# Local attention in groups of 128 queries instead of 96: small TensorE tiles per chunk, sums taken after the values, one turn at the end

## The chip, the cores and the metric

The kernel runs on one core of a Trainium2 chip. The metric is device microseconds of one execution, from three runs of the kernel before. One further execution was profiled; all rows below come from it.

## What is computed

Three stages follow one another: chunked local attention, a two-matrix MLP, and a gated MLP. Cut to what matters:

```python
B, H, S, D = 4, 8, 768, 64;  chunk, left, right, n_mem = 32, 16, 8, 8
for c in range(S // chunk):                     # 24 chunks of 32 queries per batch and head
    k_full = concat(mem_k, k[c*32-16 : c*32+40])        # 8 + at most 56 keys = 64
    v_full = concat(mem_v, v[c*32-16 : c*32+40])
    s = q[chunk] @ k_full.T / sqrt(D);  a = exp(s - max(s))
    out[chunk] = (a / (sum(a) + 1e-9)) @ v_full
x = out as [3072 tokens, 512]
g = s * relu(x @ w_in)**2 + b;  y = g @ w_out           # d_ff 2048
out = (silu(y @ w_gate) * (y @ w_val)) @ w_out2         # d_ff 1536
```

All inputs and the output are float32.

## The kernel before

**Tiling.** The 3072 tokens are cut into 8 blocks of T = 384 for the first MLP. A block takes 4 attention groups of GQ = 96 queries, so there are 32 groups. A group covers 3 chunks; it loads 96 query rows and GK = 128 key and value rows (8 memory rows and 120 of the sequence), all 8 heads side by side, from DRAM in pieces of 64 floats (256 bytes).

**One group.** `stage_transposes` turns keys (4 transposes, two heads each, 128 columns) and queries (4 transposes, 96 columns) into PSUM. `stage_keys` copies both to SBUF. `stage_scores` makes 8 products, one per head, 64 rows deep, 96 queries against all 128 keys; a head of even number sits in TensorE's rows 0 to 63, one of odd number in rows 64 to 127. `stage_max` adds a mask that leaves each query its own 64 keys and takes the maximum, head by head. `stage_exp` takes the exponential head by head on ScalarE, with the sum. `stage_normalise` divides on VectorE. `stage_probs` turns the probabilities (8 transposes of 96 columns), `stage_probs_copy` copies them, `stage_values` multiplies by the values (8 products, 128 rows deep, 64 output rows each, two heads one above the other in PSUM). `stage_x` writes the result as two float32r halves, high and low.

**Passes.** A float32 product goes to TensorE as two passes, each with its own weight load; so 8 products are 16 records in a profile. A float32 transpose is one. The MLPs use float32r, three products for one (L422 to L424).

**The first MLP.** For each block and each of 16 slices m of d_ff: an up step (12 matmuls of 384 columns into `hp`), then relu, square, scale and rounding on ScalarE and VectorE, and a down step (12 matmuls into four banks `acc`). Block 0 is cut: m 0 to 5 of block 0, then all of block 1, then the rest of block 0, then blocks 2 to 7. Each slice's weights (1 MB) are loaded once and split into two float32r parts, mainly on VectorE (`split`); all 16 stay in SBUF.

**The order** is made when the program is built. `START` is the order of TensorE's first steps, written out by hand (T transposes, S scores, A probabilities, V values, U up, D down). Later groups are put between up and down steps by `tick`. `LOADS` is the order of the first transfers on the one DMA queue (SP). `MOVED` names the steps that may run on either of ScalarE and VectorE and are put on the second choice. `Plan.run` orders every engine's instructions from given lengths; TensorE keeps the order of the calls. On the chip each engine runs its list in order and waits for semaphores. The first nine groups are in `START`; the probabilities of the first 8 groups lie in three buffers lent from the weights. In PSUM attention has two banks `a`, and at the start also the `acc` banks.

The lines the steps below touch: L283 to L298 loads, L313 and L315 transposes, L333 scores, L354 maximum, L366 exponential, L376 division, L385 and L402 probabilities and values, L415 the low half, L222 and L224 copies, L233 and L238 weight loads, L482 and L484 rounding in the first MLP.

## Time and profile before

| what | value |
|---|---|
| median of 3 runs | 1258.27 us (1257.05 to 1258.80) |
| the profiled execution | 1259.23 us, its span 1257.5 us |
| TensorE busy | 1225.2 us, 97% of the span |
| VectorE, ScalarE busy | 761.3 us (61%), 625.9 us (50%) |
| granted TensorE clock, mean | 0.995 |
| moved by DMA | 171.84 MB in 157138 packets, 97512 of them under 512 bytes |

A busy share is taken over the whole span, though the stages have different limits. The time of a TensorE step is read here from start to start, since each matmul's record is longer than the distance to the next (they are pipelined). "PEld" is the weight load that belongs to a matmul.

### The profile page before, as it was taken

What the parts mean: (1) busy time and instruction counts of PE and PEld (TensorE: products, weight loads), DVE (VectorE), ACT (ScalarE), POOL (GpSimd) and SP (SyncE); (2) the same over time, 40 slices, a digit from 0 to 9 for tenths busy, and PEclk for the clock granted to TensorE, in tenths of its full rate; (3) what the DMA queues carried; (4) which work ended last, traced back from release to release, by engine and by line L of the source; (5) the groups of instructions that cost most, each with busy time, mean ns of one, the idle gap of its engine ahead of it and who ended that gap; (6) DMA issues with size and microseconds to landing.
All of it is one profiled execution on the core that took longest, in us unless ns stands there. A gap on an engine that the chain in (4) does not pass through costs nothing.

```text
span 1257.5 us, 22202 instructions
## 1 busy us (share of the span) xinstructions
PE 1225.2 (97%) x8496; PEld 1162.8 (92%) x8496; DVE 761.3 (61%) x1846; ACT 625.9 (50%) x1596; POOL 0.7 (0%) x6
## 2 busy tenths in 40 slices
PE   5899999999999999999999999999999999999998
PEld 4788999999999999999999999999999999999997
DVE  6989865444444444454569886667964447744444
ACT  6967455454454545453348554455543335433332
POOL 0000000000000000000000000000000000000000
PEclk9889999999999999999999999999999999999999
DMA  9973232222112122120263455567665558545532
GB/s 192 270 207 114 72 75 55 61 43 57 39 32 64 32 64 44 36 68 1 87 233 109 141 186 187 188 229 283 244 219 190 185 185 297 206 184 187 188 120 93
DMA packets 157138, 171.84 MB, mean 137 GB/s; under 512 B 97512, under 2 KB 128744, under 8 KB 155496
## 3 DMA queue, kind: packets, MB, share of 16 engines
q1 hardware_dynamic: 157032, 170.42, 42.7%
q8 instruction: 67, 1.10, 0.4%
q14 instruction: 39, 0.32, 0.1%
HBM read 122.42 MB, written 47.97 MB: 136 GB/s over the span
## 4 chain that ended last, share of the span: by engine, by line
PE 89%; DVE 6%; ACT 2%; DMA 1%; issue 1%; SPq 0%; DVEq 0%; ACTq 0%
PE hp L422 7%; PE acc L423 6%; PE acc L422 6%; PE acc L424 6%; PE hp L423 6%; PE hp L424 6%; PE chain_a L422 5%; PE chain_a L423 5%; PE chain_a L424 5%; PE oacc L423 5%; PE oacc L422 5%; PE oacc L424 5%; PE chain_b L423 4%; PE chain_b L422 4%; PE chain_b L424 4%; PE psS L333 3%
## 5 line engine op out<-in xcount | busy, mean ns | idle before, releaser
L422 PE MATMUL hp<-xhi,w_first 128*128 128x384 f32 x512 | 177.9, 347 | 0.0
L423 PE MATMUL acc<-glo,w_first 128*128 128x384 f32 x512 | 172.3, 337 | 4.7 <-DVE glo L482 4.5
L422 PE MATMUL acc<-ghi,w_first 128*128 128x384 f32 x512 | 173.0, 338 | 2.1 <-ACT kq L222 1.3
L424 PE MATMUL acc<-ghi,w_first 128*128 128x384 f32 x512 | 172.1, 336 | 0.0
L423 PE MATMUL hp<-xlo,w_first 128*128 128x384 f32 x512 | 171.5, 335 | 0.1
L424 PE MATMUL hp<-xhi,w_first 128*128 128x384 f32 x512 | 171.3, 335 | 0.0
L610 ACT ACTIVATE kept<-chain_a 128x256 f32<-128x256 f32 x216 | 83.0, 385 | 159.5 <-PE chain_a L424 132.2
L462 DVE SCALAR_TENSOR_TENSOR r<-r,s_sb 128x384 f32<-128x384 f32 x99 | 61.0, 616 | 143.2 <-ACT r L451 143.0
L451 ACT ACTIVATE r<-hp 128x384 f32<-128x384 f32 x116 | 56.7, 488 | 126.2 <-PE hp L424 125.2
L422 PE MATMUL oacc<-w_down,ghi 128*128 128x512 f32 x288 | 114.1, 396 | 0.1
L423 PE MATMUL oacc<-w_down,ghi 128*128 128x512 f32 x288 | 114.1, 396 | 0.0
L424 PE MATMUL oacc<-w_down,glo 128*128 128x512 f32 x288 | 112.0, 389 | 0.0
L366 ACT ACTIVATE sc<-sc,mx 96x128 f32<-96x128 f32 x256 | 99.3, 392 | 22.6 <-DVE mx L361 22.5
L484 DVE SCALAR_TENSOR_TENSOR glo<-r,b_sb,ghi 128x384 fp32r<-128x384 f32 x99 | 61.1, 617 | 68.5 <-ACT ghi L473 68.3
L423 PEld LDWEIGHTS acc<-glo,w_first 128*128 128x128 f32 x512 | 96.7, 189 | 6.1 <-DVE glo L482 5.5
L422 PEld LDWEIGHTS acc<-ghi,w_first 128*128 128x128 f32 x512 | 96.6, 189 | 3.4 <-ACT kq L222 1.5
L422 PEld LDWEIGHTS hp<-xhi,w_first 128*128 128x128 f32 x512 | 96.4, 188 | 3.0
L423 PEld LDWEIGHTS hp<-xlo,w_first 128*128 128x128 f32 x512 | 96.5, 188 | 0.3 <-DVE xlo L415 0.3
L424 PEld LDWEIGHTS acc<-ghi,w_first 128*128 128x128 f32 x512 | 96.7, 189 | 0.0
L424 PEld LDWEIGHTS hp<-xhi,w_first 128*128 128x128 f32 x512 | 96.2, 188 | 0.0
L627 DVE TENSOR_TENSOR v<-v,g 128x256 f32<-128x256 f32 x144 | 60.9, 423 | 56.5 <-ACT g L623 54.6
L473 ACT ACTIVATE ghi<-r,b_sb 128x384 fp32r<-128x384 f32 x95 | 58.3, 614 | 52.6 <-DVE r L462 51.5
(135 smaller groups left out, 2891.1 us busy)
## 6 DMA issues: line engine op xcount, KB each, us to landing
y<-ops_dram SPq DMA_DIRECT2D x48, 512.0 KB
ops_dram<-y SPq DMA_DIRECT2D x24, 512.0 KB
sum_dram<-o SPq DMA_DIRECT2D x48, 256.0 KB
o<-sum_dram SPq DMA_DIRECT2D x12, 1024.0 KB
yhi<-ops_dram_hi SPq DMA_DIRECT2D x12, 768.0 KB
ylo<-ops_dram_lo SPq DMA_DIRECT2D x12, 768.0 KB
raw_first<-in_moe_w_in_dram SPq DMA_DIRECT2D x16, 512.0 KB
raw_first<-in_moe_w_out_dram SPq DMA_DIRECT2D x16, 512.0 KB
```

Source lines behind the costliest of these rows:

```text
L333: nc.tensor.matmul(banks[e][:GQ, j * GK:(j + 1) * GK], qt[r, j, :], kt[r, j, :], start=True, stop=True)
L366: nc.scalar.activation(out=sc[:, h, :], in_=sc[:, h, :], func=AF.Exp, bias=mx[:, h:h + 1], scale=SCALE, accum_out=sm[:, h:h + 1],)
L422: nc.tensor.matmul(o, whi, xhi, start=first, stop=False, skip_group_check=onto)
L423: nc.tensor.matmul(o, whi, xlo, start=False, stop=False, skip_group_check=onto)
L424: nc.tensor.matmul(o, wlo, xhi, start=False, stop=last, skip_group_check=onto)
L451: nc.scalar.activation(out=r, in_=hp, func=AF.Relu)
L462: nc.vector.scalar_tensor_tensor(out=r, in0=r, scalar=s_sb[:, 0:1], in1=r, op0=ALU.mult, op1=ALU.mult)
L473: nc.scalar.activation(out=hi, in_=r, func=AF.Identity, bias=bias)
L484: nc.vector.scalar_tensor_tensor(out=lo, in0=r, scalar=bias, in1=hi.bitcast(F32), op0=ALU.add, op1=ALU.subtract)
L610: nc.scalar.activation(out=t, in_=st2[n]["A"], func=AF.Copy)
L627: nc.vector.tensor_tensor(out=v, in0=v, in1=g, op=ALU.mult)
```

## The change

A group now has 128 queries (4 chunks), so a block of 384 tokens takes 3 groups and there are 24. Keys come as 128 rows `ka` and 24 + 8 rows `kb`, and are transposed in pairs `ka`, `kb`; the copy to SBUF lays out, for each chunk, its own 64 keys (`stage_keys_copy`, twice for the sequence and twice for the memory rows). Scores: for each pair of heads, chunk and head a product of 64 rows by 32 queries by 64 keys, so 32 of them, in eight places of TensorE (2 by rows, 4 by columns). No mask is needed; the maximum is taken over four heads at once, then subtracted, and one exponential covers the group (two groups, g3 and g7, keep the old form with bias). Probabilities are turned 4 times 128 columns. Values: each chunk's 64 value rows are loaded to their own place (8 transfers of 56 rows by 4 heads, a column of ones beside each head), and 32 products give output and sum together, queries on partitions. The output is divided by the sum (`stage_sums`, `stage_normalise`), and a last step turns it (`stage_turn`, 4 transposes of 128 columns). `START`, `LOADS`, `MOVED` are new, and `VISITS` names the half steps at which a group's six TensorE steps come.

```diff
-GQ = 96
-GK = 128
+GQ = 128
 START = (
-    "T0 S0 T1 S1 T2 S2 A0 V0 A1 T3 S3 V1 T4 A2 V2 S4 T5 A3 V3 S5 U T6 A4 S6 V4 T7 U S7 A5 V5 T8 "
-    "D U D A6 U V6 D U D U A7 V7 D U D S8 U"
+    "Q0 T0 S0 Q1 T1 A0 V0 X0 S1 Q2 T2 A1 S2 V1 A2 X1 V2 X2 Q3 T3 U S3 U Q4 A3 D T4 U S4 D V3 "
+    "U Q5 A4 D X3 V4 U T5 D S5 U D A5 X4 V5 D X5 U "
 )
+VISITS = {
+    (True, 0): (-3, 3, 5, 7, 8, 15),
...
+    (False, 0): (-4, -2, 0, 2, 3, 10),
...
 LOADS = (
-    "K0 K1 W0 V0 K2 K3 W2 V2 K4 V1 K5 W1 V4 V3 W3 K6 K7 V5 W9 W4 K8 W5 V8 V6 W6 V7 W8 W10 W7 W11"
+    "W0 K0 W2 K1 V0 W1 K2 V1 W4 V2 K3 W3 K4 W5 W8 W6 V3 K5 V4 W7 W9 V5 W10 "
 )
...
-    T = 4 * GQ
+    T = 3 * GQ
...
+            for c in range(NC):
+                a = s0 + c * CHUNK - LEFT
...
+                        nc.sync.dma_start(
+                            out=tv[r0:r0 + n, c, :, 0:D],
+                            in_=v[b, e:H:2, first:first + n, :].rearrange("h s d -> s h d"),
+                        )
...
+    def stage_keys(g, early):
+        ka, kb = loaded[g]["ka"], loaded[g]["kb"]
+        n = REST + NMEM
+        for i in range(2):
...
+            for jj in range(2):
+                c = slice((2 * i + jj) * P, (2 * i + jj + 1) * P)
+                nc.tensor.transpose(kps[:, jj, 0:P], ka[:, c], ident)
+                nc.tensor.transpose(kps[:, jj, P:], kb[:n, c], ident[:n, :n])
...
         for j in range(NP):
-            for e in range(2):
-                r = slice(e * D, (e + 1) * D)
-                nc.tensor.matmul(
-                    banks[e][:GQ, j * GK:(j + 1) * GK], qt[r, j, :], kt[r, j, :], start=True, stop=True
-                )
+            for c in range(NC):
+                cs = slice(c * CHUNK, (c + 1) * CHUNK)
+                for e in range(2):
+                    r = slice(e * D, (e + 1) * D)
+                    nc.tensor.matmul(banks[e][cs, j], qt[r, j, cs], kt[r, j, c], start=True, stop=True)
...
-            nc.vector.tensor_tensor_reduce(
-                out=sc[:, h, :], in0=banks[e][:GQ, j * GK:(j + 1) * GK], in1=mask, scale=1.0,
-                scalar=BIG, op0=ALU.add, op1=ALU.max, accum_out=mx[:, h:h + 1],
-            )
+        nc.vector.tensor_reduce(
+            out=staged[g]["mx"][:, e].rearrange("p j o -> p (j o)"), in_=ps, op=ALU.max, axis=AX.X
+        )
...
+        nc.scalar.activation(out=sc, in_=sc, func=AF.Exp, scale=SCALE)
...
-        for h in range(H):
-            j, e = divmod(h, 2)
-            nc.tensor.matmul(vps[e * D:(e + 1) * D, j, :], tv[:, h, :], at[:, h, :], start=True, stop=True)
+        for j in range(NP):
+            for c in range(NC):
+                cs = slice(c * CHUNK, (c + 1) * CHUNK)
+                for e in range(2):
+                    r = slice(e * KC, (e + 1) * KC)
+                    nc.tensor.matmul(banks[e][cs, j], at[r, j, cs], tv[r, c, j], start=True, stop=True)
...
+    def stage_turn(g):
+        on = staged.pop(g)["on"]
+        vps = bank(ps_h, "h", f"psO{g}").rearrange("p (j s) -> p j s", j=NP)
+        for j in range(NP):
+            nc.tensor.transpose(vps[:, j, :], on[:, j].rearrange("p e d -> p (e d)"), ident)
```

On TensorE in the first MLP, a later group's key step stood between a down and an up step like this before (`ident` is the identity, `x4` four in a row; sizes are output rows by columns):

```order
L424 MATMUL acc_1258<-ghi,w_first_1625 128x384
L313 MATMUL psT_0_1864<-ident,k_920 128x128 x4
L315 MATMUL psT_1_1865<-ident,q_923 128x96 x4
L422 MATMUL hp<-xhi_402,w_first_1148 128x384
```

and like this now:

```order
L500 MATMUL hp<-xhi_411,w_first_1502 128x384
L361 MATMUL psK_0_2370<-ident,ka_2065 128x128
L362 MATMUL psK_0_2370<-ident,kb_2066 128x32
L361 MATMUL psK_0_2370<-ident,ka_2065 128x128
L362 MATMUL psK_0_2370<-ident,kb_2066 128x32
L361 MATMUL psK_1_2375<-ident,ka_2065 128x128
L362 MATMUL psK_1_2375<-ident,kb_2066 128x32
L361 MATMUL psK_1_2375<-ident,ka_2065 128x128
L362 MATMUL psK_1_2375<-ident,kb_2066 128x32
L498 MATMUL acc_2203<-ghi,w_first_1463 128x384
```

The queries have moved to a step of their own, and transposes from all 128 rows alternate with transposes from 32 rows (`kb`).

On TensorE in a scores step, one product per head stood in a row before, even heads to bank 0 and odd heads to bank 1:

```order
L333 MATMUL psS_0_209<-kq_0_205,kq_0_207 96x128
L333 MATMUL psS_1_210<-kq_0_205,kq_0_207 96x128
L333 MATMUL psS_0_209<-kq_0_205,kq_0_207 96x128
L333 MATMUL psS_1_210<-kq_0_205,kq_0_207 96x128
```

and now, of 32 rows the first eight (four chunks, even and odd head of one pair):

```order
L390 MATMUL psS_0_1148<-kt_1110,qt_986 32x64
L390 MATMUL psS_1_1149<-kt_1110,qt_986 32x64
L390 MATMUL psS_0_1148<-kt_1110,qt_986 32x64
L390 MATMUL psS_1_1149<-kt_1110,qt_986 32x64
L390 MATMUL psS_0_1148<-kt_1110,qt_986 32x64
L390 MATMUL psS_1_1149<-kt_1110,qt_986 32x64
L390 MATMUL psS_0_1148<-kt_1110,qt_986 32x64
L390 MATMUL psS_1_1149<-kt_1110,qt_986 32x64
```

Eight products, one for each place, stand between two of the same place; before it was two.

On SP near the start, the values of group 1 and what stood behind them before (`raw_first` is a weight slice):

```order
L287 DMA v_304<-in_mem_v_dram 8x8x64
L295 DMA v_304<-in_v_dram 120x8x64
L287 DMA k_330<-in_mem_k_dram 8x8x64
L295 DMA k_330<-in_k_dram 120x8x64
```

and now, with the values of group 2 after the next weight slice:

```order
L325 DMA v_305<-in_mem_v_dram 8x4x64
L336 DMA v_305<-in_v_dram 56x4x64 x4
L325 DMA v_305<-in_mem_v_dram 8x4x64
L336 DMA v_305<-in_v_dram 56x4x64 x4
L256 DMA s_sb<-in_moe_s_dram 128x1
L256 DMA b_sb<-in_moe_b_dram 128x1
L239 DMA raw_first_436<-in_moe_w_in_dram 128x4x256
L244 DMA raw_first_436<-in_moe_w_out_dram 128x1024
L336 DMA v_190<-in_v_dram 56x4x64 x8
```

A group's values are 8 to 12 transfers instead of 2 or 3, and `v_190` is the tile that group 0 used, so its second filling stands behind the values step of group 0.

## Rows read from the trace of the kernel before

**Rows 1.** Windows: five stretches, busy time of each engine, granted clock, DMA.
```profile
0.00:40.84 40.84, 26.25 (x240) 22.08 (x240) 29.96 (x136) 28.32 (x92) 0.70 (x6) 0.96 1.01 211
40.84:120.00 79.16, 69.86 (x464) 65.49 (x463) 73.93 (x145) 61.53 (x145) 0.00 (x0) 0.94 0.74 200
120.00:600.00 480.00, 480.00 (x3400) 466.26 (x3399) 239.83 (x738) 238.19 (x700) 0.00 (x0) 1.00 0.20 49
600.00:690.00 90.00, 87.20 (x516) 85.86 (x515) 65.76 (x105) 49.52 (x80) 0.00 (x0) 1.00 0.41 145
690.00:1257.50 567.50, 561.94 (x3884) 523.15 (x3883) 351.83 (x725) 248.34 (x582) 0.00 (x0) 1.00 0.54 195
```

**Rows 2.** Timeline of TensorE around one probabilities step: start, length, line, shapes, count.
```profile
422.90 0.33 PE L424 MATMUL acc<-ghi,w_first 128*128 128x384 f32 x1
...
423.42 0.34 PE L424 MATMUL acc<-ghi,w_first 128*128 128x384 f32 x1
423.60 0.82 PE L385 MATMUL psA<-ident,sc 96*128 96x96 f32 x8
424.21 0.42 PE L422 MATMUL hp<-xhi,w_first 128*128 128x384 f32 x1
...
424.64 0.34 PE L424 MATMUL hp<-xhi,w_first 128*128 128x384 f32 x1
```

**Rows 3.** Timeline of TensorE around one step of key and query transposes.
```profile
438.67 0.34 PE L424 MATMUL acc<-ghi,w_first 128*128 128x384 f32 x1
438.85 0.60 PE L313 MATMUL psT<-ident,k 128*128 128x128 f32 x4
439.28 0.49 PE L315 MATMUL psT<-ident,q 96*128 96x96 f32 x4
439.56 0.42 PE L422 MATMUL hp<-xhi,w_first 128*128 128x384 f32 x1
...
439.99 0.34 PE L424 MATMUL hp<-xhi,w_first 128*128 128x384 f32 x1
```

**Rows 4.** Timeline of TensorE around one pair of scores and values steps.
```profile
428.29 0.34 PE L424 MATMUL acc<-ghi,w_first 128*128 128x384 f32 x1
428.56 1.12 PE L333 MATMUL psS<-kq,kq 64*96 64x128 f32 x16
429.60 0.88 PE L402 MATMUL psV<-at,v 128*64 128x96 f32 x16
430.41 0.45 PE L422 MATMUL hp<-xhi,w_first 128*128 128x384 f32 x1
...
430.87 0.33 PE L424 MATMUL hp<-xhi,w_first 128*128 128x384 f32 x1
```

**Rows 5.** Timeline of weight loads: first of the scores, first of the transposes.
```profile
428.55 0.90 PEld L333 LDWEIGHTS psS<-kq,kq 64*96 64x96 f32 x16 [0.25 <-ACT ghi L473]
...
438.68 0.53 PEld L313 LDWEIGHTS psT<-ident,k 128*128 128x128 f32 x4
```

**Rows 6.** Windows of TensorE alone where that scores step begins: busy, records at work.
```profile
428.50:428.60 0.10, 0.10 (x3) 1.00 0.00 0
428.60:428.70 0.10, 0.10 (x3) 1.00 0.00 0
```

**Rows 7.** Groups of instructions by line and shape, VectorE and ScalarE.
```profile
L354 DVE CUSTOM_DVE_ANT_0 sc<-psS,mask_inner 96x128 f32<-96x128 f32 x192 | 43.1, 282 | 16.9 <-PE psS L333 16.8
L376 DVE TENSOR_TENSOR sc<-sc,rc 96x1024 f32<-96x1024 f32 x32 | 39.1, 1221 | 1.1
L615 DVE TENSOR_TENSOR v<-chain_b,kept 128x256 f32<-128x256 f32 x144 | 60.8, 422 | 37.8 <-PE chain_b L424 25.5 <-ACT ghi L222 10.1 <-ACT kept L610 1.1
L659 DVE TENSOR_TENSOR o<-oacc,o 128x512 f32<-128x512 f32 x48 | 32.2, 686 | 11.0 <-PE oacc L424 10.8
L366 ACT ACTIVATE sc<-sc,mx 96x128 f32<-96x128 f32 x256 | 99.3, 392 | 22.6 <-DVE mx L361 22.5
```

**Rows 8.** Timeline of SP: two issues of values transfers near the start.
```profile
22.00 1.13 SPq L287 DMA_DIRECT2D v<-in_mem_v_dram x1
23.17 0.33 SPq L295 DMA_DIRECT2D v<-in_v_dram x1
```

More of the change, by code (lines that the diff above doesn't have):

```diff
@@ L403, in stage_values @@
+    def stage_turn(g):
+        on = staged.pop(g)["on"]
+        vps = bank(ps_h, "h", f"psO{g}").rearrange("p (j s) -> p j s", j=NP)
+        for j in range(NP):
+            nc.tensor.transpose(vps[:, j, :], on[:, j].rearrange("p e d -> p (e d)"), ident)
         staged[g] = vps
@@ new lines, in plan_keys @@
+    def plan_keys(g, early):
+        t = plan.add(
+            PE, 0.60, lambda: stage_keys(g, early), [at_[g]["qk"]], take=["acc01"] if early else ["a", "a"],
+            give=[] if g < EARLY else ["qk"],
+        )
+        for i in range(2):
+            t = either(
+                f"k{g}_{i}", {ACT: 0.55, DVE: 0.60}, lambda e, i=i: stage_keys_copy(e, g, i, False), [t],
+                take=["kt"] if i == 0 else (),
+            )
+            t = either(
+                f"m{g}_{i}", {ACT: 0.26, DVE: 0.20}, lambda e, i=i: stage_keys_copy(e, g, i, True), [t],
+                give=[] if early else ["a"],
+            )
+        if early:
+            plan.rings["acc01"].append(t)
+        at_[g]["t"] = at_[g]["qt"], t
```

360 lines of the change are left out of this document (204 added, 156 removed), and 20 rows, old and new, of tables (MOVED, VISITS).

## The prediction

> **What bounds the kernel now.** I read the windows by stretch first. From 120 to 600 us, where attention for later groups runs between the steps of the first MLP, TensorE is busy 480.0 of 480.0 us and VectorE and ScalarE about half the time [rows 1]. What attention costs there is TensorE's time alone, and it counts fully. From 690 us on nothing of the change is left. Before 120 us it is otherwise: up to 40.84 us, when the first up step starts, TensorE idles 14.6 us and the DMA engines are busy all the time (share 1.01); from there to 120 us it idles 9.3 us and the clock averages 0.94 of full speed, some 4.7 us more, while VectorE works 73.9 of 79.2 us [rows 1]. So two sums are needed: TensorE's price of a group, and what the start gives or takes.
>
> **A group before.** In the timeline I take the distance from the last MLP matmul ahead of a step to the third one behind it, and subtract three undisturbed distances, 423.42 - 422.90 = 0.52 us [rows 2]. Probabilities: 424.64 - 423.42 - 0.52 = 0.70 us [rows 2]. Transposes: 439.99 - 438.67 - 0.52 = 0.80 [rows 3]. Scores and values, back to back: 430.87 - 428.29 - 0.52 = 2.06 [rows 4]. Together 3.56 us, and 32 groups make 113.9 us.
>
> **Two prices behind it.** A column of a float32 pass costs 0.84 ns: four key transposes of 128 columns take 439.28 - 438.85 = 0.43 us [rows 3]. By it the two kinds of transpose steps are 0.65 and 0.75 us of streaming, each with about 0.05 around it. Scores are 16 passes of 128 columns, values 16 of 96, 3.01 us in single file; the measured 2.06 is less, so two passes, in different places of the array, run at once: 1.51 us. The other 0.55 us belongs to three changes, from full array to half rows, to half columns, and back: 0.185 us each. One sees them: the first scores pass starts 0.27 us after the last MLP matmul instead of 0.17 [rows 4], and its weight load starts with it at 428.55 [rows 5], whereas the first transposes' load, where the array stays whole, runs ahead of its pass, at 438.68 against 438.85 [rows 3, 5]. So a change costs 0.10 us of waiting and then a load that could not go ahead.
>
> **A group after.** Queries, probabilities and the turn are each 4 transposes of 128 columns in the whole array: 0.43 + 0.05 = 0.48, together 1.44 us. Scores are 64 passes of 64 columns, 3.44 us in single file; in eight places at once 0.43, and two changes (each now stands alone between MLP steps) 0.37: 0.80. Values, 65 columns, 0.81. No row shows eight at once; the bounds are two at once as now (1.72 + 0.37 = 2.09) and eight. I take eight, because the trace shows the array overtaking in program order: a product's two passes stand next to each other and use the same place, and yet two scores passes are at work in the first 0.05 us, and no third until after 428.70 (the third record in those windows is the MLP matmul) [rows 6]; the second must be the other head's.
>
> Keys: 4 x (128 + 32) columns are 0.54 us. But `ka` uses all 128 rows and `kb` 32, in turn, so the array changes eight times. No row shows 128 rows to 32; the bounds are nothing and 0.185 each, and the nearest rows, from 128 rows to 64 and back, pay [rows 4]. The waiting part is 0.10; a transpose's load takes at most 0.08, since probabilities with loads of 128 columns pass every 0.61/8 [rows 2]. I take 0.155: 1.24 us. Keys 0.54 + 1.24 + 0.03 = 1.81 us.
>
> The Trainium skill, "TensorEngine Tiling (Array Packing)", section "Tiling Modes", says that a change of tiling mode, not of place alone, makes TensorE drain, and lists 32 by 128 as a mode of its own. That speaks for the eight changes; the rows on scores and values agree for the modes that occur there, and no row has the mode of `kb`.
>
> Sum: 1.44 + 1.81 + 0.80 + 0.81 = 4.86 us, 24 groups 116.6: 2.7 us more than before. What fewer columns and fewer groups save is eaten by changes of mode: twelve in a group (eight in keys, two each in scores and values) where there were three.
>
> **VectorE and ScalarE after 120 us** have half their time free [rows 1], so what they are spared there is worth nothing. New waits: in the first group of a block VISITS puts the probabilities two half steps behind the scores, 24 matmuls of 0.173 us or 4.15 us, for two maxima, two subtractions of 128x256 from PSUM (0.42 each [rows 7]), an exponential and the hops between engines, about 3.3 us. That fits; if VectorE's rounding work stands in between, up to 0.5 us for the five or six such groups; it lies in the range.
>
> **The start.** Transfers before the first up step: before, up to V3 in LOADS, six K of 448 KB, five V of 256, three W of 1024: 7040 KB. After, up to V2: four W, three K of 576, three V of some 465: 7220 KB. The DMA engines were full [rows 1], so the first up step moves by about +1 us (40.84 to 42). POOL gets copies of memory rows, hidden behind the same transfers. Behind it: VectorE's work of one group was 8 x 0.28 + 1.22 and 0.55 for the low half, 4.0 us; now six operations of 128x256 at 0.42 and a low half of 128x512 at 0.69, 3.2 us [rows 7]. START held nine groups and holds six, so VectorE, nearly full there, is spared 36 - 19 = 17 us; ScalarE has one exponential instead of eight of 0.39 [rows 7]. What that can give TensorE is at most the 14 us it loses between 40.84 and 120. Values of groups 3 to 5 stand behind some 9 MB of other transfers, which at the 211 GB/s of the first stretch take over 40 us, so waits for them will take the place of some of VectorE's; I take half, 7. Together -6, bounds -15 and +9.
>
> **Sum.** 1259.2 us (the profiled execution) + 2.7 - 6 = 1255.9; the median of the runs lies 0.9 below that execution, so 1255.0 us.
>
> **Rivals.**
> (a) *Keys don't pay for changes*: then they take 0.54 + 0.05 up to 0.70 (if `kb`'s load bounds), 1.15 less, 24 times 27.6, of which the first groups' part is waited away: about 24. 1231 us. For it: transposes are another kind of pass than products. Against: every change of mode in the trace is paid. 0.16.
> (b) *Fewer than eight places at once*: the engine must look past 28 passes and loads to reach the eighth place, where it had to look past two. With four at once scores and values cost 0.43 more each, 24 x 0.87 = 21 us: 1276; with two, 24 x 2.6 = 62: 1317. It is slower than before as soon as the two take 0.26 us more a group, i.e. below some six places. 0.22, of which 0.06 for two.
> (c) *Values come late*: 30 transfers of values stand before V2 in SP's list, issues are seen at 0.33 to 1.13 us [rows 8], so 10 to 34 us of 36, and they write to rows of 65 floats. Behind the slow end stand K3, W3 and all that follows; the first up step would come some 9 us late: 1263. It decides from about 0.9 us an issue. 0.10.
>
> The Trainium skill, "TensorE: Matmul & The Clock Gate", section "Part 3: Packing small matmuls", says that matmuls start and end in strict program order. Then a product's two passes could not be overtaken and scores would take 32 x 0.054 + 0.37 = 2.1 us, the two-place end of (b). [Rows 6] speak against it; it is the 0.06.
>
> **How the numbers follow.** The forecast has 0.52. Its own range is 1243 to 1263: keys' changes at 0.10 to 0.185 give -11 to +6, the start -9 to +15 about my value, and they rarely add. A difference under 0.2%, 2.5 us, can't be told from no change here. Of the 0.52, 0.32 is faster by more, 0.11 within, 0.09 slower. (a) is faster; (b) slower; of (c) 0.02 is faster, 0.02 within, 0.06 slower. Faster 0.50, same 0.13, slower 0.37. The range must reach into (a) and over (b) with four places: 1230 to 1279.
>
> **What would show it.** In the timeline between 120 and 600 us: a keys step of 1.8 us between MLP matmuls (0.6 to 0.7 is rival a), its loads not ahead of their passes; scores and values of 0.8 us each (1.2 or 2.1 is rival b); queries, probabilities and turn 0.48. TensorE busy all of that stretch. First up step at 41 to 43 us (50 is rival c); idle time from there to 120 us of 5 us instead of 9.3, and VectorE below 85%. Wrong would be the sum if TensorE waits after 120 us, or if the second MLP moves by more than 1 us.

## The result and the profile after

The changed kernel takes 1269.07 us (median; 1267.83 to 1273.27), the kernel before, run beside it, 1257.66 (1256.46 to 1258.8): ratio 1.0097, 95% interval 1.0071 to 1.0122. It is slower by about 1%. 1255.0 was forecast, with 1230 to 1279 as its range: the time lies in the range, but on the slower side, where a faster kernel was forecast. The profiled execution has a span of 1266.8 us, 9.3 more than before.

Windows by stretch of the kernel after (us, then busy time of PE, PEld, DVE, ACT and POOL with counts, granted clock, DMA share, GB/s), to be laid beside [rows 1]:

```profile
0.00:40.84 40.84, 23.64 (x402) 16.68 (x410) 27.12 (x50) 14.77 (x23) 8.14 (x20) 1.00 0.82 195
40.84:120.00 79.16, 71.64 (x774) 64.97 (x772) 68.94 (x113) 45.13 (x77) 7.54 (x12) 0.94 0.74 203
120.00:600.00 480.00, 480.00 (x4781) 453.92 (x4780) 213.02 (x442) 169.65 (x327) 9.99 (x24) 1.00 0.22 55
600.00:690.00 90.00, 90.00 (x638) 88.47 (x637) 60.92 (x104) 46.86 (x78) 0.00 (x0) 1.00 0.41 144
```

TensorE is still busy all the time from 120 to 600 us, and now also to 690 us, and VectorE and ScalarE have become idler, as their share of the new work is smaller. So behind the start the price of a group on TensorE is nearly all that counts, and it can be read as in [rows 2 to 4]: from the last MLP matmul ahead of a step to the third behind it, less 0.52 us. Timelines of TensorE, one step of each kind (start, length, line, shapes, count): queries, keys, scores, values.

```profile
313.71 0.34 PE L500 MATMUL acc<-ghi,w_first 128*128 128x384 f32 x1
313.88 0.60 PE L350 MATMUL psQ<-ident,q 128*128 128x128 f32 x4
...
314.67 0.34 PE L500 MATMUL hp<-xhi,w_first 128*128 128x384 f32 x1
...
324.56 0.34 PE L500 MATMUL hp<-xhi,w_first 128*128 128x384 f32 x1
324.73 0.27 PE L361 MATMUL psK<-ident,ka 128*128 128x128 f32 x1
324.94 0.24 PE L362 MATMUL psK<-ident,kb 32*128 32x32 f32 x1
325.11 0.33 PE L361 MATMUL psK<-ident,ka 128*128 128x128 f32 x1
...
326.86 0.34 PE L500 MATMUL acc<-ghi,w_first 128*128 128x384 f32 x1
...
333.06 0.34 PE L500 MATMUL acc<-ghi,w_first 128*128 128x384 f32 x1
333.33 0.86 PE L390 MATMUL psS<-kt,qt 64*32 64x64 f32 x64
...
334.57 0.34 PE L500 MATMUL hp<-xhi,w_first 128*128 128x384 f32 x1
...
344.91 0.34 PE L500 MATMUL hp<-xhi,w_first 128*128 128x384 f32 x1
345.18 0.86 PE L455 MATMUL psV<-v,at 64*32 64x65 f32 x64
...
346.43 0.33 PE L500 MATMUL acc<-ghi,w_first 128*128 128x384 f32 x1
```

Queries 314.67 - 313.71 - 0.52 = 0.44 us; keys 326.86 - 324.56 - 0.52 = 1.78; scores 334.57 - 333.06 - 0.52 = 0.99; values 346.43 - 344.91 - 0.52 = 1.00. Over all steps between 200 and 620 us the medians are 0.446, 1.787, 0.993 and 0.995, and 0.451 and 0.445 for probabilities and turn: 5.117 us a group, 24 x 5.117 = 122.8 us, against 113.9 before: +8.9, where +2.7 was forecast.

**Where the 9.3 us are.** I counted the first MLP's matmuls, 3072 of them, in both traces. The 250th starts at 110.99 us before and at 115.39 after, +4.4. Up to there the old kernel had paid for 8 groups and for transposes and scores of a ninth (8 x 3.56 + 0.80 + 1.06 = 30.3 us), the new one for 6 groups (30.7), so +4.0 of the 4.4 is not the groups' price. The last one ends at 689.51 and 698.84, +9.3. Between the two lie 92.1 us of attention after (18 groups) and 113.9 - 30.3 = 83.6 before, +8.5; the other -3.6 is a gain behind the 250th matmul. About 1 us of it still belongs to the start: the kernel before waits 0.98 us at 114.91 us, just behind its 250th matmul. The rest is at the end, where the kernel before waited twice for VectorE, and the kernel after not at all. Timeline of TensorE in the kernel before, the only two rows between 600 and 690 us with idle time ahead (in brackets, with its releaser):

```profile
625.81 0.45 PE L422 MATMUL acc<-ghi,w_first 128*128 128x384 f32 x1 [0.81 <-DVE y L224]
634.84 0.45 PE L423 MATMUL acc<-glo,w_first 128*128 128x384 f32 x1 [1.81 <-DVE glo L482]
```

From the second MLP's first matmul to the end of the span it is 568.12 us before and 568.14 after. So: groups +8.9, start (up to the 250th matmul) +4.0, behind it -3.6, sum +9.3.

### The profile page after: what moved, and what is told of

Same layout as the page of the kernel before. It is cut to its first block, busy times and chain, and to the rows that moved or that the text cites. A ratio compares the mean times of both kernels' runs of the same rounds, so it can differ in the third digit from the quotient of the medians.

```text
span 1266.8 us, 25728 instructions
## 1 busy us (share of the span) xinstructions
PE 1236.2 (98%) x10512; PEld 1155.7 (91%) x10512; DVE 730.9 (58%) x1446; ACT 532.2 (42%) x1097; POOL 25.7 (2%) x56
## 4 chain that ended last, share of the span: by engine, by line
PE 91%; DMA 3%; SPq 3%; DVE 2%; ACT 1%; issue 0%; DVEq 0%; ACTq 0%
PE acc L498 7%; PE hp L498 7%; PE acc L499 7%; PE acc L500 7%; PE hp L500 7%; PE hp L499 7%; PE chain_a L498 5%; PE chain_a L499 5%; PE chain_a L500 5%; PE oacc L499 5%; PE oacc L498 5%; PE oacc L500 5%; PE chain_b L499 4%; PE chain_b L498 4%; PE chain_b L500 4%; SPq L284 2%
## 5 line engine op out<-in xcount | busy, mean ns | idle before, releaser
L498 PE MATMUL acc<-ghi,w_first 128*128 128x384 f32 x512 | 178.0, 348 | 3.0 <-DVE ghi L551 2.7
L500 PE MATMUL acc<-ghi,w_first 128*128 128x384 f32 x512 | 172.4, 337 | 0.0
L538 DVE SCALAR_TENSOR_TENSOR r<-r,s_sb 128x384 f32<-128x384 f32 x93 | 57.5, 618 | 114.8 <-ACT r L527 114.4
L527 ACT ACTIVATE r<-hp 128x384 f32<-128x384 f32 x104 | 51.1, 492 | 171.3 <-PE hp L500 160.3
L560 DVE SCALAR_TENSOR_TENSOR glo<-r,b_sb,ghi 128x384 fp32r<-128x384 f32 x93 | 58.0, 624 | 46.8 <-ACT ghi L549 40.4
L691 DVE TENSOR_TENSOR v<-chain_b,kept 128x256 f32<-128x256 f32 x144 | 61.0, 423 | 37.6 <-PE chain_b L500 25.4
L711 DVE TENSOR_TENSOR glo<-v,ghi 128x256 fp32r<-128x256 f32 x144 | 60.7, 422 | 37.0 <-ACT ghi L228 36.9
```

What stands on the lines that cost most here:

```text
L498: nc.tensor.matmul(o, whi, xhi, start=first, stop=False, skip_group_check=onto)
L500: nc.tensor.matmul(o, wlo, xhi, start=False, stop=last, skip_group_check=onto)
L527: nc.scalar.activation(out=r, in_=hp, func=AF.Relu)
L538: nc.vector.scalar_tensor_tensor(out=r, in0=r, scalar=s_sb[:, 0:1], in1=r, op0=ALU.mult, op1=ALU.mult)
L560: nc.vector.scalar_tensor_tensor(out=lo, in0=r, scalar=bias, in1=hi.bitcast(F32), op0=ALU.add, op1=ALU.subtract)
L691: nc.vector.tensor_tensor(out=t, in0=st2[n]["B"], in1=st2[n].pop(f"a{i}"), op=ALU.add)
```

## The experiments

Ratios are to the kernel before, run on the same chip beside each; that of the changed kernel is 1.0097.

### What the keys step pays for

Keys sorted, in `stage_keys`:

```diff
-            for jj in range(2):
-                nc.tensor.transpose(kps[:, jj, 0:P], ka[:, c], ident)
-                nc.tensor.transpose(kps[:, jj, P:], kb[:n, c], ident[:n, :n])
+        for j in range(NP):
+            nc.tensor.transpose(staged[g]["k", j // 2][:, j % 2, 0:P], ka[:, j * P:(j + 1) * P], ident)
+        for j in range(NP):
+            nc.tensor.transpose(
+                staged[g]["k", j // 2][:, j % 2, P:], kb[:n, j * P:(j + 1) * P], ident[:n, :n]
+            )
```

> The keys step transposes the four full tiles of ka first and then the four 32-row tiles of kb, where the changed kernel alternates them: two changes of array size in a step in place of eight. Theory A (each change of array size has a price of about 0.15 us, whatever stands on its two sides): the step, 1.79 us in the changed kernel, falls to 0.45 (four full transposes, as the queries step shows) plus 0.15 (four small ones) plus 2 x 0.15 = 0.9 us; 0.89 us x 24 groups = 21 us, so about 1248 us. Rival (the small transposes are dear by themselves, in whatever order they come): the step stays at 1.79 us and the time at 1269 us. A step between 1.1 and 1.6 us would say that both hold in part.

Measured: 1256.33 us, ratio 0.9974 (0.9963 to 0.9986). Timeline of its keys step:

```profile
319.61 0.34 PE L501 MATMUL hp<-xhi,w_first 128*128 128x384 f32 x1
319.79 0.60 PE L360 MATMUL psK<-ident,ka 128*128 128x128 f32 x4
320.32 0.43 PE L362 MATMUL psK<-ident,kb 32*128 32x32 f32 x4
...
321.14 0.33 PE L501 MATMUL acc<-ghi,w_first 128*128 128x384 f32 x1
```

1.01 us: the same eight transposes, six changes of array size fewer, 0.78 us less, so 0.13 us a change. That is a lower bound: in the single records the small transposes, one behind the other, start 0.06 us apart, where 32 columns at 0.84 ns are 0.03, so they have a price of their own here that takes back part of what the changes cost. The rival, that small transposes are dear in any order, falls all the same. The span fell by 13.6 us and not by 24 x 0.78 = 18.7; 18 x 0.78 = 14.0, so the six groups of the start gave nothing. Their saving is seen as a wait: the first 45 us have 5.0 us of idle time ahead of the probabilities' transposes in place of 2.4.

Keys through the full array, for groups 6 to 23 (`kb` is then one tile whose other 96 rows are zero):

```diff
+                if g < EARLY:
                     nc.tensor.transpose(kps[:, jj, P:], kb[:n, c], ident[:n, :n])
+                else:
+                    nc.tensor.matmul(kps[:, jj, P:], kb[:, c], ident[:, :n], start=True, stop=True)
```

> For groups 6 to 23 the tile kb keeps 96 rows of zeros under its 32 rows, and its four turns are products of all 128 rows with the first 32 columns of the identity, so the keys step never leaves the full array; the order stays alternating, and groups 0 to 5 stay as they were. Theory A (the price belongs to the change of array size): a step of these 18 groups takes 0.45 us for ka and 4 x (0.03 to 0.11) us for kb, 0.6 to 0.9 us in place of 1.79; 18 x 0.9 to 1.2 = 16 to 21 us, so 1248 to 1253 us. Rival (alternating between a product of 128 columns and one of 32, or between two inputs, is what costs): 1.79 us and 1269 us stay.

Measured: 1258.54 us, ratio 0.9998 (0.9986 to 1.001), the step 1.20 us. Direction right, size wrong: a plain float32 product has two passes, each with a load of 128 columns, so the four cost (1.20 - 0.45) / 4 = 0.19 us each without any change of size. A way around a change is only worth something if it doesn't bring passes.

Two tiles of 80 rows in place of 128 and 32:

```diff
-    REST = SPAN - P
+    KA = (SPAN + NMEM) // 2
+    REST = SPAN - KA
...
-                nc.tensor.transpose(kps[:, jj, 0:P], ka[:, c], ident)
+                nc.tensor.transpose(kps[:, jj, 0:KA], ka[:KA, c], ident[:KA, :KA])
```

> The 160 rows of keys of a group (152 of its own and 8 of memory) lie in two tiles of 80 rows in place of one of 128 and one of 32, so that all eight transposes of the keys step use the same array size and none stands between two sizes; the bytes loaded are the same. Theory A (a change costs about 0.13 us, as the sorted step gave: 1.79 - 1.01 = 0.78 us for six of them): the step takes 8 x 80 columns x 0.84 ns = 0.54 us, up to 0.7 us with loads that are not covered; against 1.79 us that is 1.1 to 1.25 us for each of the 18 groups behind the start, 20 to 22 us, about 1247 us (the six groups of the start gave nothing in the sorted kernel). Rival (the full-array products of the run on full arrays took 1.20 us a step without any change, so eight transposes have a floor near 0.15 us each, changes or not): 1.2 us a step, 11 us, about 1258 us.

Measured: 1250.0 us, ratio 0.9936 (0.992 to 0.9952): faster than both kernels. Timeline of its keys step:

```profile
317.84 0.34 PE L501 MATMUL hp<-xhi,w_first 128*128 128x384 f32 x1
318.02 0.23 PE L362 MATMUL psK<-ident,ka 80*128 80x80 f32 x1
318.09 0.23 PE L363 MATMUL psK<-ident,kb 80*128 80x80 f32 x1
318.16 0.23 PE L362 MATMUL psK<-ident,ka 80*128 80x80 f32 x1
...
318.50 0.23 PE L363 MATMUL psK<-ident,kb 80*128 80x80 f32 x1
...
318.97 0.33 PE L501 MATMUL acc<-ghi,w_first 128*128 128x384 f32 x1
```

A transpose every 0.07 us, 80 columns at 0.84 ns, and 0.61 us for the step: eight changes fewer, 1.18 us less, 0.15 us a change. The mechanism that the prediction gave for the keys is shown: from the 250th matmul to the first MLP's last it is 583.45 us in the changed kernel and 562.17 here, 21.3 less, and 18 x (1.787 - 0.606) = 21.3. The rule of "TensorEngine Tiling (Array Packing)" in the Trainium skill, section "Tiling Modes", that a change of mode drains, agrees for 128 rows to 32 too; its price here is 0.13 us by the sorted step and 0.15 by this one.

### What scores and values pay for

In the single records of the scores step at 302.93 us of the changed kernel, the 64 passes start thus: 32 in four rounds of eight, 6.7 ns from one to the next and 0.080 us, then twice 0.056 us from round to round (by place, too, passes of one place start 0.056 us apart); then a gap, and the other 32 take 0.40 us, about 12 ns each. The eight places do work at once, but only for the first half.

By place, and the same products twice, in `stage_scores`; values are untouched in both and stay at 1.00 us:

```diff
-        for j in range(NP):
-            for c in range(NC):
-                for e in range(2):
+        for c in range(NC):
+            for e in range(2):
+                for j in range(NP):
                     nc.tensor.matmul(banks[e][cs, j], qt[r, j, cs], kt[r, j, c], start=True, stop=True)
```

```diff
-        for j in range(NP):
+        for j in [*range(NP), *range(NP)]:
```

> The 32 products of the scores step are issued place by place, the four products of one place one behind the other, where the changed kernel goes round all eight places; the values step is left as it is and is the control. In the changed kernel the 64 passes of a step start within 0.643 us: the first 32 in rounds of eight every 0.056 us, the others at 11.7 ns each. Theory B (TensorE holds some 32 passes ready at a time, places don't wait for each other, and beyond those the rate at which instructions arrive, 11.7 ns a pass, is the limit): only four places are in sight at first, each works through its eight passes in 8 x 0.056 = 0.45 us while the rest arrive, and the last place, which arrives from 0.3 us on, ends at about 0.75; the step takes 1.0 to 1.2 us where it took 0.99, +0 to +5 us in all. Rival 1 (strict order: a pass that waits for its place holds up all behind it): 64 x 0.056 = 3.6 us, the step 3.9 us, +70 us, about 1339 us. Rival 2 (arrival alone sets the time from the first pass on): 0.99 us, no change.

> The scores step issues its 32 products twice over into the same places (the second set writes the same sums again); the values step is left as it is and is the control. Theory B (after the first 32 passes the arrival of instructions at 11.7 ns a pass is the limit): 64 more passes take 64 x 11.7 ns = 0.75 us, the step 0.99 + 0.75 = 1.74 us, 24 groups +18 us, about 1287 us. Rival (the places are the limit, and a round of eight takes 0.056 us wherever it stands, the slow second half of the step being an effect of its end): 8 rounds x 0.056 = 0.45 us, the step 1.44 us, +11 us, about 1280 us. Rival 2 (the step's 0.99 us is mostly the change into and out of the small array, and passes are almost free): under 0.3 us, +7 us or less.

Measured: 1295.88 and 1285.54 us, one execution each, so these two carry the price of a step and no verdict on the time. Timelines of a scores step, first by place, then twice:

```profile
311.75 0.34 PE L500 MATMUL acc<-ghi,w_first 128*128 128x384 f32 x1
312.02 2.40 PE L390 MATMUL psS<-kt,qt 64*32 64x64 f32 x64
...
314.81 0.34 PE L500 MATMUL hp<-xhi,w_first 128*128 128x384 f32 x1
```

```profile
312.50 0.34 PE L500 MATMUL acc<-ghi,w_first 128*128 128x384 f32 x1
312.77 1.48 PE L390 MATMUL psS<-kt,qt 64*32 64x64 f32 x128
...
314.64 0.34 PE L500 MATMUL hp<-xhi,w_first 128*128 128x384 f32 x1
```

Twice: 314.64 - 312.50 - 0.52 = 1.62 us, 0.63 more for 64 passes, 9.8 ns each. That lies between the arrival of instructions (0.75) and the places (0.45), nearer to the first; a step that is mostly change of mode falls. What sets the rate isn't shown: each pass has its own weight load, and in the single records the loads start as far apart as the passes, so a limit on loads would look the same as one on the arrival of instructions. By place: 314.81 - 311.75 - 0.52 = 2.54 us, which none of the three theories gave. The records tell why: the first place's passes start at 0.268, 0.348, 0.404, 0.460 and 0.515 us behind the last MLP matmul, and the next place's first pass at 0.521, right behind the fifth; so on through all eight, 0.253 us a place. So, as the records read, a place takes about four passes, running and waiting, and where one more comes for it, it and all behind it stand, whatever places are free. Theory B was right that passes overtake and wrong that some 32 are in sight whatever their place: it is eight times four, and the changed kernel's rounds of eight places fill just that. The rule that matmuls run in strict program order, weighed in the prediction ("TensorE: Matmul & The Clock Gate" in the Trainium skill, section "Part 3: Packing small matmuls"), holds inside a place, not between places.

### What the start pays for

W4 behind V2 and K3 in `LOADS`; that and the sorted keys; and K0, K1 and values ahead of weights too:

```diff
-    "W0 K0 W2 K1 V0 W1 K2 V1 W4 V2 K3 W3 K4 W5 W8 W6 V3 K5 V4 W7 W9 V5 W10 "
+    "W0 K0 W2 K1 V0 W1 K2 V1 V2 K3 W4 W3 K4 W5 W8 W6 V3 K5 V4 W7 W9 V5 W10 "
```

```diff
+    "K0 W0 K1 V0 W2 K2 V1 W1 V2 K3 W4 W3 K4 W5 W8 W6 V3 K5 V4 W7 W9 V5 W10 "
```

> The fifth weight tile of the first MLP (W4) is asked for behind the values and the keys of the third group, where the changed kernel asks for it ahead of both; all else stays. In the changed kernel ScalarE stands idle from 31.97 to 36.72 us for W4's landing (L778), with the ready exponential of group 2 behind it in its in-order list, and the first up step of the MLP starts at 45.91 us. Theory C (this wait is on the path that sets the start): the wait goes, the values of group 2 land earlier too, the first up step comes at 42 to 43 us and the whole at about 1265 us, 3 to 4 us under the changed kernel. Rival (the values of group 2 or the turn behind them are late anyway, the wait is covered): the first up step stays at 45 to 46 us, the time at 1268 to 1269 us. Rival 2 (W4 is now late for the MLP's own steps): TensorE waits for it between 50 and 80 us and the time grows by 1 to 4 us.

> Both edits at once: the keys step sorted (four full transposes, then four small ones) and W4 asked for behind V2 and K3. With the sorted step alone the time was 1256.3 us; the wait of the probabilities' transposes for the exponentials in the first 45 us had grown from 2.4 to 5.0 us there, by about what the sorted steps of the first groups had saved. Theory C (ScalarE's wait for W4 holds the start, so the six early groups' price is hidden behind it): with the wait gone both are gained, the first up step at 39 to 41 us and 1250 to 1252 us. Rival (the start is held by the landing of values, whatever W4 does): 1255 to 1257 us.

> As the run before it, and the keys of group 0 are asked for ahead of W0, those of group 1 and the values of group 0 ahead of W2, and V2 and W1 swapped round with V1, so that the first transposes need not wait for W0. In the changed kernel the first transposes start at 8.61 us, in the kernel before at 5.21 us. Theory C': the attention chain of the first groups is what holds the start, so the first transposes at about 5.2 us bring the first up step forward by another 2 to 3 us, 1248 to 1250 us. Rival (the weights W0 to W2 are then late for ScalarE and VectorE, which prepare them in order, and the first up step waits for those): no gain over the run before, or 1 to 3 us lost.

Measured: 1272.14 us, ratio 1.0106 (1.009 to 1.0123); 1258.82, 0.9996 (0.9985 to 1.0008); 1259.27, 1.0001 (0.9991 to 1.001). The first can't be told from the changed kernel, as its rival had it; the other two are slightly slower than sorted keys alone. In the changed kernel ScalarE's wait for W4 and TensorE's behind it are plain. Timelines, ScalarE and TensorE:

```profile
36.72 1.12 ACT L778 ACTIVATE t_first<-raw_first 128x1024 f32<-128x1024 f32 x1 [4.76 <-DMA raw_first<-in_moe_w_out_dram]
37.74 0.61 ACT L432 ACTIVATE qk<-qk 128x512 f32<-128x512 f32 x1
```

```profile
38.41 1.12 PE L439 MATMUL psA<-ident,qk 128*128 128x128 f32 x4 [2.37 <-ACT qk L432]
```

Yet theory C falls, and so does C'. The first up step came at 45.49, 43.6 and 41.9 us in place of 45.91 (46.4 with sorted keys), but the 250th matmul at 122, 119.7 and 119.0 in place of 115.4 (115.9). What was gained before the first up step was given back behind it: in the first of the three as waits of 5.1 us at 89 us and 3.9 us at 105, where the changed kernel's longest there is 2.7.

The last long wait of the start is the one for `ghi` near 100 us: ScalarE waits for a store of first partial sums. The two runs that follow took it to be one that stands behind value transfers on SyncE. Two kernels with the keys in tiles of 80 rows take it on: values (and their memory rows) asked for from GpSimd's queue, and the four stores from ScalarE's:

```diff
-                        nc.sync.dma_start(
+                        nc.gpsimd.dma_start(
                             out=tv[r0:r0 + n, c, :, 0:D],
```

```diff
-        nc.sync.dma_start(out=(y_dram[t] if m == M1 - 1 else part_dram)[:, i, :], in_=y_t.pop((t, i)))
+        (nc.sync if m == M1 - 1 else nc.scalar).dma_start(out=(y_dram[t] if m == M1 - 1 else part_dram)[:, i, :], in_=y_t.pop((t, i)))
```

> The kernel with keys in two tiles of 80 rows, and the values asked for from GpSimd's queue in place of SyncE's; the weights, queries, keys and stores stay on SyncE's. Theory D (transfers pace the start by their bytes, whoever asks for them): the values no longer hold up what stands behind them on SyncE, but share the same DMA engines; the 250th of the first MLP's matmuls stays between 114 and 117 us (116.9 in the kernel with 80-row tiles) and the time at 1248 to 1251 us. Theory E (the order on SyncE's queue holds the start: the stores of the first partial sums stood behind ten value transfers from 93.4 to 101.7 us, and ScalarE and then TensorE waited for them 3.6 and 4.9 us): the 250th matmul comes at 110 to 113 us and the time is 1244 to 1247 us. Rival (the requests are slower from GpSimd, or the values now overtake weights): later by 1 to 6 us, 1251 to 1256 us.

> The kernel with keys in two tiles of 80 rows, and only the four stores of the first partial sums are asked for from ScalarE's queue, right behind the copies that make them, in place of SyncE's, where the fourth stands behind ten value transfers. Theory E (those stores hold the tiles that ScalarE needs for the next gate, and so TensorE's 4.9 us wait at 98 us): that wait shrinks to under 2 us, the 250th matmul of the first MLP comes 3 to 4 us earlier, 113 to 114 us, and the time is 1246 to 1247 us. Theory D (bytes pace the start; the stores only queue in the DMA engines instead): the wait goes to another place, the 250th matmul stays within 1.5 us and the time at 1249 to 1250 us.

Measured: 1261.74 us, 1.0025 (1.0012 to 1.0038), later than any of the three theories said, with the first up step at 66.5 us. The price of a request alone isn't the reason: GpSimd takes some 0.65 us for one. But GpSimd also copies the memory rows of the first groups, in order with its requests, and stands 5.7, 7.3 and 7.7 us (up to 18.11, 30.55 and 43.11 us) until those rows have landed, with the other values behind them; TensorE then waits 9.6 us for values at 49.90 us. So this run says little on theory E. And 1248.33, 0.9913 (0.9881 to 0.9945), the fastest of all by its median, though it can't be told from the 80-row tiles alone (0.992 to 0.9952). TensorE's waits there, first with 80-row tiles alone, then with the stores moved:

```profile
101.07 0.69 PE L499 MATMUL acc<-ghi,w_first 128*128 128x384 f32 x1 [4.93 <-DVE ghi L552]
```

```profile
79.42 0.30 PE L391 MATMUL psS<-kt,qt 64*32 64x64 f32 x2 [1.82 <-ACT kt L229]
80.68 1.17 PE L391 MATMUL psS<-kt,qt 64*32 64x64 f32 x62 [0.97 <-ACT kt L229]
...
101.15 0.44 PE L499 MATMUL acc<-ghi,w_first 128*128 128x384 f32 x1 [1.79 <-DVE ghi L552]
```

The wait shrank from 4.93 to 1.79 us, others grew at 79 us, and the 250th matmul came at 116.5 in place of 116.9. Theory E falls for its size, and its premise falls too. Timelines of SyncE and ScalarE with 80-row tiles alone:

```profile
91.57 1.33 SPq L584 DMA_DIRECT2D part_dram<-y  x3
101.68 0.35 SPq L584 DMA_DIRECT2D part_dram<-y  x1
99.42 0.49 ACT L528 ACTIVATE r<-hp 128x384 f32<-128x384 f32 x1 [3.58 <-DMA part_dram<-y]
```

ScalarE goes on at 99.42 us, before the fourth store is even asked for. What it waited for is the landing of one of the first three, asked for ahead of those value transfers: some 7.7 us after the first of them was asked for. With the stores moved the first is asked for at 92.73 us and the same wait ends at 99.2, still 6.5 us later. So most of that time lies in the landing, whichever queue asks.

Value transfers taken away or shortened, in groups 2 to 5:

```diff
-            for c in range(NC):
+            for c in range(1 if 2 <= g < EARLY else NC):
```

```diff
+                    if 2 <= g < EARLY:
+                        n = min(n, WIN // 4)
```

> Of groups 2 to 5 only the first of the four value windows is loaded; the other three keep what an earlier group left there, so the output is wrong for these groups: it leaves out 24 of their 32 value transfers of 112 KB a pair, some 1.3 MB of the 23.3 MB that the start moves in its first 112 us, and 24 issues of SyncE's queue. All else is the changed kernel. Theory D (the start is set by the transfers, not by TensorE or ScalarE: the DMA engines are 0.73 to 0.83 busy at about 200 GB/s until 112 us, and a wait removed early came back later): 1.3 MB at 210 GB/s is 6 us, so the time falls by 4 to 7 us, to 1262 to 1265 us. Rival (the chain of ScalarE and VectorE through the groups sets the start): within 1 us of the changed kernel, 1268 to 1270 us.

> As the run before it, but all four windows of groups 2 to 5 are asked for with 14 of their 48 rows each (the rest of the rows keep what was there, so the output is wrong for these groups): nearly as few bytes as with one window, and as many transfers to issue as in the changed kernel. Theory D by bytes: the same gain as the run before, 4 to 7 us. Theory D by issues (SyncE's queue, which stood 6 to 10 us on the eight to ten issues of one group's values, is the limit): no gain here, 1267 to 1270 us, while the run before gains. Rival (neither): both stay at 1268 to 1270 us.

Measured: 1265.61 us, 1.0049 (1.0034 to 1.0065), and 1265.56, 1.0053 (1.0036 to 1.007); 0.0048 and 0.0044 below the changed kernel's ratio, 5.5 to 6 us (3.5 by the medians, 2.2 by the profiled spans). A window has 56 rows, not 48, so a quarter of the bytes is left in both. The same gain with 24 requests fewer or with all of them: so the requests taken away were worth nothing here, and the first up step has nothing to do with it (48.4 and 47.7 us, later than in the changed kernel). That it is the bytes themselves isn't shown, for the waits and the clock changed with them. Windows from the first up step to the 250th matmul in the kernel before, the changed one and the first of these two:

```profile
40.84:110.99 70.15, 61.83 (x419) 57.78 (x418) 65.02 (x135) 54.98 (x136) 0.00 (x0) 0.93 0.80 211
45.91:115.39 69.48, 63.30 (x683) 57.69 (x682) 60.39 (x99) 41.76 (x72) 7.54 (x12) 0.93 0.75 203
48.40:112.76 64.36, 60.49 (x682) 54.71 (x682) 59.35 (x97) 41.55 (x71) 8.64 (x12) 1.00 0.63 184
```

TensorE idles 3.9 us in place of 6.2 and the granted clock is 1.00, where the changed kernel has 0.93 (the second run: 3.8 us and 0.97). A clock of 0.93 over 69.5 us is worth up to 4.9 us, an estimate from that row, so the clock alone could be the gain.

The reverse, each of these transfers twice, into the same place and then into spare memory; and VectorE's subtraction four times in the first six groups:

```diff
-                        nc.sync.dma_start(
-                            out=tv[r0:r0 + n, c, :, 0:D],
+                        for _ in range(2 if 2 <= g < EARLY else 1):
+                            nc.sync.dma_start(
+                                out=tv[r0:r0 + n, c, :, 0:D],
```

```diff
+                        for to in (tv, spare) if 2 <= g < EARLY else (tv,):
+                            nc.sync.dma_start(
+                                out=to[r0:r0 + n, c, :, 0:D],
```

```diff
-        nc.vector.tensor_tensor(
-            out=scores_to(g)[:, :, e], in0=staged[g]["s"][e],
+        for _ in range(4 if g < EARLY else 1):
+            nc.vector.tensor_tensor(
+                out=scores_to(g)[:, :, e], in0=staged[g]["s"][e],
```

> The changed kernel with every value transfer of groups 2 to 5 asked for twice (the same bytes into the same place): 1.8 MB more than the 23.3 MB that the start moves, and 32 more issues, the mirror of the two runs that took 1.3 MB away and gained 0.45% of the time. Theory D (the start answers to the bytes that it moves): 1.8 MB at 210 GB/s is 8.5 us; in proportion to those runs, +5 to +9 us, 1274 to 1278 us. Rival (the bytes there were not the limit; those runs gained because single waits fell well): within 2 us of the changed kernel, 1267 to 1271 us.

> The changed kernel with every value transfer of groups 2 to 5 asked for a second time into spare memory that nobody reads, so that no transfer waits for another one's landing: 1.8 MB and 32 issues more. Theory D (the start answers to the bytes that it moves): between the proportion to the runs that took 1.3 MB away, +5 us, and 1.8 MB at 210 GB/s, +8.5 us: 1274 to 1278 us. Rival (bytes are not the limit): within 2 us of the changed kernel, 1267 to 1271 us.

> The changed kernel with VectorE's subtraction of the maxima issued four times in place of once in the first six groups (the same result again): 30 more operations of 0.416 us, 12.5 us more for VectorE before 112 us. The prediction took 17 us that VectorE is spared there to be worth 7 us. Theory F (VectorE's time in the start is worth 0.4 of itself): +5 us, about 1274 us. Theory D (transfers set the start and VectorE's work hides behind them): under +2 us, 1268 to 1271 us. More than 8 us would say that the chain of one group, which these operations lengthen by 2.5 us, sets the start link by link.

Measured: 1334.9 us, 1.0604 (1.0585 to 1.0623). Here each second transfer waited until the first, to the same rows, had landed. SyncE's waits up to 180 us (total, times, longest):

```profile
SPq L337 <- DMA v<-in_v_dram: 66.9, 34, 7.6
```

So that run tells the price of a chain of landings, 2 us each, and nothing of bytes. Into spare memory: 1299.24 us, 1.0321 (1.0303 to 1.0338), 28 us above the changed kernel by the ratios, where bytes gave 5 to 8.5 and the rival nothing. SyncE's timeline:

```profile
31.44 0.50 SPq L339 DMA_DIRECT2D v<-in_v_dram x1
31.99 0.85 SPq L339 DMA_DIRECT2D spare<-in_v_dram x1
32.94 0.50 SPq L339 DMA_DIRECT2D v<-in_v_dram x1
33.48 0.81 SPq L339 DMA_DIRECT2D spare<-in_v_dram x1
```

32 more requests at 0.8 us are 26 us of SyncE's queue, and the 250th matmul came 28 us late (143.5). The DMA engines' share fell to 0.61 behind the first up step, from 0.75, so it isn't bytes that held this run. Added requests cost what they take on that queue (into spare memory, which is DRAM, 0.8 us each, where the same request into SBUF beside it takes 0.5); 24 requests taken away gave no more than shorter ones did. The VectorE run: 1273.16 us, 1.0111 (1.0096 to 1.0126), 1.8 us above the changed kernel by the ratios, with intervals that overlap, but 4.1 by the medians, and in the profiled executions span and 250th matmul are both 5.1 us later: 12.5 us of VectorE's time in the start are worth some 2 to 5 us, and theory F, which said 5, isn't excluded.

## Why the prediction was wrong

**Right.** The keys step: 1.81 us forecast, 1.79 measured, and the sorted and the 80-row runs show that the eight changes are what it pays for, at 0.13 to 0.15 us each (0.155 taken, bounds 0 and 0.185); rival (a) fell. Queries, probabilities and turn: 0.48 forecast, 0.45 measured, 0.1 us a group less in all. TensorE without a wait after 120 us, and the second MLP unmoved, as said.

**The term that was mis-sized: scores and values.** 0.80 and 0.81 forecast, 0.99 and 1.00 measured. The step said "in eight places at once 0.43" for 64 passes; in the trace it is 0.24 us for the first 32 passes and 0.40 for the rest. What is left of the 0.99, 0.35 us, is close to the 0.37 for two changes. That the array reaches the eighth place was right, and rival (b) was asked the wrong question: not how far the array looks ahead, but how fast new passes start once the four that each place takes are used up, about 12 ns each, for a cause that stays open. [Rows 4] show 16 scores passes in 1.04 us, so nothing in the rows of before asked for passes at that rate. 0.38 us x 24 = 9.1 us, of which 2.9 come back from keys and transposes: the 6.2 between +2.7 and +8.9. With it the sum would have been 1261, slower than before already.

**The term with the wrong sign: the start.** -6 forecast, +4.0 measured. Two parts. The first up step was to move by +1 and moved by 45.91 - 40.84 = +5.1: the step counted kilobytes at the old rate, but the DMA engines, which [rows 1] show full (1.01) up to 40.84 us, are at 0.82 after, with 195 GB/s in place of 211. So it is no longer set by bytes, and their order in `LOADS` matters: with sorted keys it came at 46.4 us, and at 41.9 with W4 later and K0 and values earlier. Behind it 7 us were to be gained from 17 us of VectorE's time. TensorE's idle time between the first up step and the 250th matmul did fall, but only from 8.3 to 6.2 us. The step failed first at the 17: up to the 250th matmul VectorE was busy 95.0 us before and is 91.6 us after, 3.4 less. Attention takes less of it, but some 4 us more of the weights' preparation and 3 us more of the first MLP's relu, square and rounding now run there (by the single records), which the step did not count; it is ScalarE that was spared, from 83.3 to 57.3 us. What a microsecond of VectorE's time is worth, the step "I take half", stays open between 0.15 and 0.4 by the VectorE run. Rival (c), values late by their requests, comes closest, though not by its reason: the 22 value requests ahead of V2 (30 with V2's own eight) took 0.42 us each on average, not 0.9, and its 50 us for the first up step is too much; but SyncE stands 6.3 and 10.1 us over the eight value requests of groups 2 and 3, of which the requests themselves are 3.4 us each time and the rest is waiting between them. Timeline of SyncE in the changed kernel, against [rows 8]:

```profile
30.67 6.34 SPq L336 DMA_DIRECT2D v<-in_v_dram x8
49.26 10.12 SPq L336 DMA_DIRECT2D v<-in_v_dram x8
```

**The term that was left out: the end.** What VectorE and ScalarE are spared after 120 us "is worth nothing", the prediction said; [rows 1] already show 2.8 us that TensorE waits between 600 and 690 us, and in the kernel after those waits are gone; VectorE, relieved, is the likely cause, but `MOVED` is new too and no run tells the two apart. With the 0.98 us at 114.91 us it makes the -3.6.

Misses of +6.2, +10.0 and -3.6 make the 12.6 us between a forecast of 3.3 us less and the 9.3 us more. Neither miss alone decides the sign safely: with the start as forecast the kernel would have ended about level with the one before, with scores and values as forecast some 3 us slower. That the time lies in the stated range at all is due to its width, made for the rivals (a) and (b), neither of which came about as described.

**What stays open.** What exactly holds the first 112 us. Earlier weights, an earlier first up step and stores on another queue moved waits and not the time; fewer value bytes gained 2 to 6 us with or without their requests, together with a higher granted clock; more requests cost 28 us. That fits a start in which several chains end close to each other, but no run shows which chain it is, and none separates the transfers from the clock. The 250th matmul of a single profiled execution also moves by some 3 us between kernels that differ little (114.9 in the run by place, though its scores take 1.5 us more each), so only the timed runs carry a verdict here.

## What to carry to other kernels

Small matmuls in many places of the array are cheap only in a short burst: count how many each place gets, and price those beyond about four at the rate measured for them (10 to 12 ns a pass of 64 columns here), not at the 7 ns that eight places would allow (0.056 us for eight passes). Split an odd remainder so that all pieces use the same array size (80 and 80, not 128 and 32); where that can't be done, sort the pieces. And a saving in a stage that waits for something else is worth nothing: sorted keys gave 18 groups' worth, not 24. Before a wait is given a cause, look at when the awaited request was issued: one issued after the wait ended can't be it.

## What the runs showed of the hardware

A place of the array takes about four float32 passes, running and waiting, and one more for it holds up everything behind it: the next place's first pass starts at 0.521 us, 6 ns behind the fifth of the place before. With that room used up, passes of 64 columns start every 9.8 to 12 ns. And a wait in the start can cost more than its idle time: behind the 4.93 us at 101 us, in the kernel with 80-row tiles, MLP matmuls stand 0.32 us apart for some time (102.54, 102.86, 103.18 us), where 0.173 is usual. The granted clock there is 1.00 from 95 to 100 us, in which TensorE works 1.1 of 5 us, 0.59 from 100.5 to 103 us, so mostly the lower of its two levels, and 0.91 over 100 to 120 us:

```profile
102.54 0.52 PE L499 MATMUL acc<-ghi,w_first 128*128 128x384 f32 x1
102.86 0.52 PE L500 MATMUL acc<-glo,w_first 128*128 128x384 f32 x1
103.18 0.52 PE L501 MATMUL acc<-ghi,w_first 128*128 128x384 f32 x1
```
